# Adding two of the three chords of VectorE's exponentials in an accumulating DMA

## The chip, the cores and the metric

One core of a Trainium2 chip runs the whole program. The metric is the device time of one execution in microseconds (us). The kernel before takes 757.84 us, the median of 3 runs (757.2 to 758.05). One more execution was taken with the hardware profiler; its span, from the first to the last instruction, is 754.6 us, and every duration below comes from it.

## The reference: one transformer block

2048 tokens of width 512 pass through an attention with 32 heads of width 16 and then through a gated feed-forward layer of width 1792, each behind a layer norm and with its input added back:

```python
def _A_ref(x, wqkv, wo):
    qkv = (x @ wqkv).reshape(B, S, 3, H, Dh).transpose(2, 0, 3, 1, 4)
    q, k, v = qkv[0], qkv[1], qkv[2]
    scores = jnp.einsum("bhqd,bhkd->bhqk", q, k) * (Dh ** -0.5)
    p = _softmax(scores, axis=-1)
    o = jnp.einsum("bhqk,bhkd->bhqd", p, v)
    return o.transpose(0, 2, 1, 3).reshape(B, S, D) @ wo

def _B_ref(x, w_gate, w_up, w_down):
    h = _sigmoid(x @ w_gate) * (x @ w_up)
    return h @ w_down

h = x + _A_ref(_layernorm(x), A_wqkv, A_wo)
out = h + _B_ref(_layernorm(h), B_w_gate, B_w_up, B_w_down)
```

The heads are narrow, so the exponentials are what there is most of: 32 x 2048 x 2048 of them.

## The kernel before, and what sets its order

**Units and tiles.** The scores are computed transposed, keys on the 128 partitions and queries along the free axis. A *unit* is 128 x 512 exponentials of one head: two key tiles by 256 queries, or in the first blocks one key tile by 512 queries. There are 2048 units. A *tile* is what one step of the main loop takes from PSUM: mostly three units, one bank each. `scores(n)` (L1085) lets TensorE write the scores of tile n; four units can use four groups of 32 rows of the array at once.

**Two engines make the exponentials.** ScalarE takes two units of a tile (three where VectorE has no room) in one ACTIVATE with Exp (L1408) and writes fp16 into a run of neighbouring *slots*: 24 slots of 512 columns in the tile `PT`, and more that other buffers lend (`xb`, `PE_`, `QTb`, `xnT`). VectorE takes one unit, the last of the tile, with `dexp_first` (L1256): one TENSOR_SCALAR turns the scores into int16 numbers, the *code*, whose bits read as fp16 are a piecewise straight approximation of the exponential, a *chord*. To come closer, the code is shifted by two constants (`CHORDS`), which gives two more chords; the wanted value is chord 0 plus chord 1 plus 1.5625 times chord 2.

**Three chords are three operands.** A tile `J` of [128, 3, 2, 512] holds the three chords of two units; there are six such buffers (`QB = 6`). After every second unit `dexp_rest` makes the two other chords, each by one integer add on GpSimd (`int64_add`, L1277, four int16 at once). The sum of the three is left to TensorE: `av` (L1233) multiplies every chord by its values, one after the other into the same accumulator, chord 2 with `Vaug2`, which is `Vaug` times 1.5625. So a unit of ScalarE costs TensorE one AV unit and a unit of VectorE costs three. An AV unit is two matmuls of 17 rows by 256 columns (one of 512 in the first blocks), and four heads run on four groups of columns at once.

**Background work.** Between scores and AV, TensorE does the projections, `wo`, the gate and up matmuls (L824) and the down matmuls (L842) of the feed-forward layer; its weights `wgu` come by DMA from SP's queue, 256 KB each, two for every two blocks of 128 columns. The last part of the feed-forward layer runs after the attention; its gate and up weights go into the `J` buffers (L1495) as these come free.

**A planner writes the order.** No scheduler is at work on the chip: every engine runs its queue in the order in which the Python code emits it. The code keeps a clock for each engine (`T["P"]`, `T["A"]`, `T["D"]`, `T["G"]` for TensorE, ScalarE, VectorE, GpSimd) and gives each operation a price in ns; a unit has an `end`, and `av` takes only units whose `end` plus 60 ns has passed on TensorE's clock (L1233 and `av_ready`). Since TensorE's queue is in order, a matmul whose operand comes later on the chip than the planner supposed holds up everything behind it. VectorE gets a unit of a tile (`split`) when its clock is not too far behind ScalarE's and a `J` buffer is free.

Of the kernel before, what the change touches and what calls it, by code (L numbers as in the profile page):

```python
# [9 lines left out]
FP16 = mybir.dt.float16  # L10
BF16 = mybir.dt.bfloat16
I16 = mybir.dt.int16
I32 = mybir.dt.int32
I64 = mybir.dt.int64
ALU = mybir.AluOpType
# [12 lines left out]
CHORDS, WEIGHT = (326, -332), 1.5625  # L28
# [114 lines left out]
def kernel(  # L143
# [11 lines left out]
    nc = tc.nc  # L155
    P = 128
    S, D = A_x.shape[1], A_x.shape[2]
# [3 lines left out]
    DC = D // P  # L161
    NG = H // 4
    NP = NG // 2
    FC = F // P
    QC = 512
# [20 lines left out]
    ZOFF = 1024 * (15 - LEVEL)  # L186
# [11 lines left out]
    dvx = main.enter_context(tc.tile_pool(name="dvx", bufs=1))  # L198
# [13 lines left out]
    Vaug = const.tile([P, NT, H, VW], BF16)  # L212
    Vaug2 = const.tile([P, NT, H, VW], BF16)
# [43 lines left out]
    for b in range(0, P, 32):  # L257
        nc.vector.tensor_tensor(out=ident_bf[b:b + 32, b:b + 32], in0=ramp[b:b + 32, 0, :],
                                in1=ramp[b:b + 32, 1, :], op=ALU.is_equal)
# [296 lines left out]
    def pool(ns, fn, *deps):  # L556
        gq.append(Job(ns, fn, deps))
        job = gq[-1]
        run_pool()
        return job  # L560
# [64 lines left out]
    def flush():  # L625
        moved = True
        while moved and (dq or aq):
            moved = False
            for q, e in ((dq, "D"), (aq, "A")):
                for job in list(q):  # L630
                    if job.ready() is not None:
                        q.remove(job)
                        job.place(e)
                        moved = True
# [576 lines left out]
    def av(limit, loose=60.0, full=False):  # L1211
        busy = [st["acc"][k] for k in acc_of(*gseq[st["cur"]])[1] if st["acc"][k] is not None]
        if any(j.end is None or j.end + LAT > T["P"] + loose for j in busy):
            return 0
        uns, rows = in_rows(av_ready(loose), ahead_ready(), limit, full)
        if not uns:
            return 0
        T["P"] = max([T["P"]] + [un.end + LAT for un in uns + busy])
        for un in uns:
            qc, g, kt, j = un.u  # L1220
            dst, halves = acc_of(qc, g)
            for k in halves:
                st["acc"][k] = None
            force(("v", kt * SPAN[qc]))
            avq.remove(un)
            c = count[qc, g, j]
            count[qc, g, j] += 1
            todo[qc, g, j] -= 1
            h = 8 * (g // 2) + 2 * j + g % 2
            w = CW[qc]  # L1230
            clears = 0 in halves
            for i in range(SPAN[qc]):
                nc.tensor.matmul(dst[32 * j:32 * j + VW, 0:w], lhsT=un.v[:, kt * SPAN[qc] + i, h, :],  # L1233
                                 rhs=un.ap[:, i * w:(i + 1) * w], start=clears and c + i == 0,
                                 stop=(todo[qc, g, j] == 0 and i == SPAN[qc] - 1), tile_position=(0, 32 * j),
                                 skip_group_check=True)
        pe_time("av", MM * rows + 4 * len(uns), 128 * len(uns))
        for un in uns:
            if un.slot is not None:
                un.slot.end = T["P"] + DRAIN  # L1240
        while st["cur"] < len(gseq) and av_last() == 0:
            finish_group(*gseq[st["cur"]])
            st["cur"] += 1
        return len(uns)

    GQ, QB = 2, 6
    quads = []
    half = []

    def dexp_first(src, u, n):  # L1250
        if not half:
            half.append(dvx.tile([P, 3, GQ, QC], I16, name="J", bufs=QB))
            quads.append([])
        J = half[0]
        k = len(half) - 1
        nc.vector.tensor_scalar(out=J[:, 0, k, :], in0=src, scalar1=ZOFF, scalar2=float(-min(CHORDS)),  # L1256
                                op0=ALU.add, op1=ALU.max)
        T["D"] = max(T["D"], sc_end[n] + LAT) + 601
        todo[u[0], u[1], u[3]] += 2
        uns = [Unit(u, J[:, s, k, :].bitcast(FP16), n, None if s else T["D"] + TAIL["D"],  # L1260
                    v=Vaug2 if s == 2 else Vaug) for s in range(3)]
        avq.extend(uns)
        half.append(uns)
        quads[-1].extend(uns)
        if k == GQ - 1:
            dexp_rest()

    def dexp_rest():
        J, quad = half[0], half[1:]
        half.clear()  # L1270
        k = len(quad)

        def words(s):
            return J[:, s, 0:k, :].rearrange("p a b -> p (a b)").bitcast(I64)

        def chord64(s):
            nc.gpsimd.int64_add(words(s), words(0), CHORDS[s - 1] * (1 + 2 ** 16 + 2 ** 32 + 2 ** 48))  # L1277
            for i in range(k):
                quad[i][s].end = T["G"] + TAIL["G"]

        def chord(s):
            nc.vector.tensor_scalar(out=J[:, s, 0:k, :], in0=J[:, 0, 0:k, :], scalar1=float(CHORDS[s - 1]),
                                    scalar2=None, op0=ALU.add)
            for i in range(k):
                quad[i][s].end = T["D"] + TAIL["D"]
        on_pool = len(st["early"]) == TQ * (NQC - 1) and all(j.end is not None for j in st["early"])
        if on_pool and not st["lib"]:
            st["lib"] = True
            T["G"] += 9000.0
        for s in (1, 2):  # L1290
            if on_pool:
                pool(150 + 192 * k, lambda s=s: chord64(s), Mark(T["D"] + TAIL["D"]))
            else:
                chain.append((70 + 133 * k, lambda s=s: chord(s)))

    def want_dve(n):

        quads[:] = [q for q in quads if any(un in avq for un in q)]
        if not blocks or not late("d"):
            return False  # L1300
        busy = sum(j.ns for j in dq if j.ready() is not None) + sum(c[0] for c in chain)
        rest = group_left() / 2.8
        if not half and len(quads) >= QB:
            return False
        if busy > 1500:
            return False
        return busy + 1900 + 1100 * (GQ - len(half[1:])) <= rest * 1100
# [2 lines left out]
        def __init__(self, tile, i, early=False):  # L1310
            self.tile, self.i, self.early, self.unit, self.end = tile, i, early, None, 0.0

    NPT, NPE = 24, 14
    PT = ptp.tile([P, NPT, QC], FP16, name="pt")
    PE_ = prep.tile([P, NPE, QC], FP16, name="pe")
    slots = [Slot(PT, i) for i in range(NPT)] + [Slot(x, i, True) for x, n in (
# [14 lines left out]
    def run_of(w):  # L1331

        best = None
        for i in range(len(slots) - w + 1):
            row = slots[i:i + w]
            if row[0].tile is row[-1].tile and not any(s.unit in avq for s in row):
                end = max(s.end for s in row)
                if best is None or end < best[0]:
                    best = end, row
        return best  # L1340

    def p_slots(w):
        while True:
            best = run_of(w)
            if best is not None:
                return best
            flush()
            if av(8, 1e12) or early_on and try_bg(1e9, 1e12):
                continue
            if half and not chain:  # L1350
                dexp_rest()
            if chain:
                pop_chain()
# [20 lines left out]
    n = -1  # L1374
    while n + 1 < len(tiles):
# [16 lines left out]
        start = max(T["A"], sc_end[n] + LAT)  # L1392
        busy = sum(j.ns for j in dq if j.ready() is not None) + sum(c[0] for c in chain)
        dable = len(tl) > 1 and busy <= 1500
        split = (dable and max(T["D"], sc_end[n] + LAT) <= start + 600 and bool(half or len(quads) < QB))
        if n > N - 12:
            end = max(T["D"], sc_end[n] + LAT) + 1900 + 600 * (GQ - len(half[1:]) if half else GQ)
            split = split and end <= start + 1330 * (N - n) - 500
        if half and half[1][0].u[:2] != tl[-1][:2]:
            dexp_rest()  # L1400
            quads[:] = [q for q in quads if any(un in avq for un in q)]
            split = split and len(quads) < QB
        wa = len(tl) - split
        more_slots()
        free_at, row = p_slots(wa)
# [68 lines left out]
    ends = [PS[:, wide["base"] + i, :] for i in range(3)] + [PS[:, last + i, :] for i in range(3)]  # L1474
    hps, gu = ends[0:n], ends[n:n + 4]
    nc.vector.tensor_scalar(out=ident2[:], in0=ident_bf[:], scalar1=2.0, scalar2=None, op0=ALU.mult)
    while any(un.n < N - 1 and un.slot is not None for un in avq):
        flush()
        av(8, 1e12)
    nc.scalar.activation(out=small.tile([P, 1], FP32, name="warm")[:], in_=eps_t[:], func=ACT.Sqrt)  # L1480
# [5 lines left out]
                             start=False, stop=False)  # L1486
    T["P"] += MM * n * NP
    tw = {}
    for i in range(QB):
        t = dvx.tile([P, 3, GQ, QC], I16, name="J", bufs=QB)[:].rearrange("p a b n -> p (a b n)")  # L1490
        n = min(3 * GQ // 2, FC - len(tw))
        f = len(tw)
        w = t[:, 0:n * 2 * DC * P].bitcast(BF16).rearrange("p (k c n) -> p k c n", k=2, c=DC)
        for k in range(2):
            nc.sync.dma_start(out=w[:, k], in_=gate_v[k][:, :, f * P:(f + n) * P])  # L1495
        for m in range(n):
            tw[f + m] = w[:, :, :, m * P:(m + 1) * P]
        if len(tw) == FC:
            break

    while avq:
        flush()
# [31 lines left out]
            for job in held:  # L1534
                job.end = 0.0
    leftover(7)
    hnl = [PT[:, k, :].bitcast(BF16) for k in range(n)]
    nc.scalar.activation(out=hnl[0], in_=hps[0], func=ACT.Identity, bias=nmr[:, 0:1], scale=rstd[:, 0:1])
    nc.vector.tensor_scalar(out=hnl[1], in0=hps[1], scalar1=mv[:, 1, 0:1], scalar2=rstd[:, 1:2],
                            op0=ALU.subtract, op1=ALU.mult)  # L1540
# [73 lines left out]
```

## Time and profile before

| | value |
|---|---|
| time, median of 3 runs | 757.84 us |
| span of the profiled execution | 754.6 us |
| start until the first exponential of ScalarE | 13.1 us |
| last exponential of ScalarE starts at | 717.2 us |
| tail (last norm and feed-forward part) | from about 720 us |
| tiles of the main loop | 695 |
| units on VectorE / on ScalarE | 619 / 1429 |
| integer adds on GpSimd | 640, 603 ns each |
| DMA moved in all | 41.65 MB, mean 55 GB/s |

In the page, the share of busy time tells which engines are full; since the stages differ, the same is read for each stage from the table of windows. Groups of instructions show how long one takes, how long its engine sat idle before it and what ended that. The chain of waits is followed back from the last instruction.

### The profile page before, as it was taken

How to read it: one execution, taken by the hardware profiler on the slowest of the kernel's cores; microseconds unless marked ns; L12 is line 12 of the kernel's file. 1: busy time of each engine (PE TensorE's matmuls, PEld its weight loads, DVE VectorE, ACT ScalarE, POOL GpSimd, SP SyncE). 2: the span in 40 equal slices, each digit the busy share in tenths (PEclk: the TensorE clock that was granted, in tenths of full speed). 3: DMA queues.
4: the chain of work that ended last, by engine and by line, in shares of the span. 5: the costliest groups of instructions: out<-in, count | busy, mean ns of one | idle time of the engine just before them, and what ended most of it. 6: DMA issues, size and time to landing. Idle time of an engine off the chain costs nothing.

```text
span 754.6 us, 27232 instructions
## 1 busy us (share of the span) xinstructions
PE 718.8 (95%) x11541; PEld 347.4 (46%) x11617; DVE 621.7 (82%) x1231; ACT 709.2 (94%) x788; POOL 396.0 (52%) x709
## 2 busy tenths in 40 slices
PE   7999998889999999999999999999999999999997
PEld 3322224444454445444555454535544455445554
DVE  7988878889978898898889688977889777899743
ACT  7989989999999999999999999999999999899952
POOL 2733546666556456655645546564555446465600
PEclk9999999999999999999999999999999999999999
DMA  7000005000123003210222122201321133003160
GB/s 238 1 1 1 1 18 153 2 3 3 30 87 99 10 10 109 78 30 10 78 59 59 36 79 58 74 22 38 99 59 30 44 93 107 10 9 105 47 203 17
DMA packets 68927, 41.65 MB, mean 55 GB/s; under 512 B 3520, under 2 KB 68800, under 8 KB 68800
## 3 DMA queue, kind: packets, MB, share of 16 engines
q1 hardware_dynamic: 68512, 39.59, 17.9%
q8 instruction: 92, 1.51, 0.9%
q14 instruction: 35, 0.29, 0.1%
q10 hardware_dynamic: 288, 0.26, 0.1%
HBM read 37.75 MB, written 2.10 MB: 53 GB/s over the span
## 4 chain that ended last, share of the span: by engine, by line
PE 74%; ACT 13%; DVE 8%; issue 4%; DMA 0%; POOL 0%; DVEq 0%; ACTq 0%; POOLq 0%
PE PS L1085 24%; PE PS L1233 23%; PE PS L824 14%; ACT pt L1408 10%; PE PS L842 6%; DVE J L1256 4%; PE PS L311 2%; PE PS L316 2%; PE PS L763 1%; ACT QTb L1408 1%; DVE xs L1151 1%; ACT xnT L1408 1%; PE PS L1560 1%; DVE st L271 1%; PE PS L305 1%
## 5 line engine op out<-in xcount | busy, mean ns | idle before, releaser
L1277 POOL INT64_ADD J<-J x640 | 377.6, 603 | 305.3 <-DVE J L1256 261.4
L1408 ACT ACTIVATE pt<-PS 128x1024 f16<-128x1024 f32 (+2 forms) x517 | 517.3, 1104 | 13.3 <-PE PS L1085 5.1
L1256 DVE TENSOR_SCALAR J<-PS 128x512 int16<-128x512 f32 x619 | 413.8, 681 | 70.1 <-PE PS L1085 42.7
L1085 PE MATMUL PS<-QT,KT 32*128 32x256 bf16 (+1 forms) x3712 | 263.8, 276 | 10.9 <-ACT pt L1408 4.9
L1233 PE MATMUL PS<-J,Vaug 128*17 128x256 f16 (+1 forms) x3546 | 243.4, 279 | 3.3 <-DVE xs L1151 1.9
L1233 PE MATMUL PS<-pt,Vaug 128*17 128x256 f16 (+1 forms) x2043 | 205.0, 279 | 2.8 <-DVE xs L1151 2.3
L1233 PEld LDWEIGHTS <-Vaug 128*17 128x17 bf16 x6204 | 139.3, 90 | 91.5 <-issue 84.4
L1085 PEld LDWEIGHTS <-KT 32*128 32x128 bf16 x3840 | 89.1, 92 | 197.2 <-issue 193.8
L824 PE MATMUL PS<-xnT,wgu 128*128 128x256 bf16 x784 | 113.7, 275 | 0.1
L1408 ACT ACTIVATE xnT<-PS 128x1024 f16<-128x1024 f32 x90 | 95.0, 1080 | 0.9 <-PE PS L1085 0.7
L824 PEld LDWEIGHTS <-wgu 128*128 128x128 bf16 x784 | 63.6, 97 | 39.6 <-issue 34.2
L1233 PE MATMUL PS<-xnT,Vaug 128*17 128x256 f16 x362 | 56.4, 274 | 0.0
L842 PE MATMUL PS<-wd,hT 128*128 128x512 bf16 x169 | 51.2, 383 | 2.5 <-issue 2.5
L1151 DVE STREAM_TRANSPOSE xs<-PS 128x256 f32<-128x256 f32 (+1 forms) x60 | 27.7, 461 | 21.9 <-PE PS L1233 21.2
L854 ACT ACTIVATE th<-PS 128x512 f32<-128x512 f32 (+1 forms) x63 | 37.4, 594 | 8.4 <-DVE hT L837 6.7
L1408 ACT ACTIVATE QTb<-PS 128x1024 f16<-128x1024 f32 x40 | 42.7, 1068 | 0.5 <-PE PS L1085 0.5
L896 DVE SCALAR_TENSOR_TENSOR hT<-th,PS 128x512 bf16<-128x512 f32 x49 | 33.3, 680 | 7.3 <-PE PS L824 7.2
L1233 PE MATMUL PS<-QTb,Vaug 128*17 128x256 f16 (+1 forms) x158 | 28.4, 275 | 0.0
L1408 ACT ACTIVATE xb<-PS 128x1024 f16<-128x1024 f32 (+2 forms) x26 | 25.6, 1030 | 2.1 <-PE PS L1085 1.1
L1122 DVE TENSOR_TENSOR o<-xs,rsum 128x128 bf16<-128x128 f32 (+1 forms) x60 | 24.4, 407 | 2.1
L1408 ACT ACTIVATE pe<-PS 128x1024 f16<-128x1024 f32 (+2 forms) x22 | 21.7, 1062 | 1.7 <-PE PS L1233 1.4
L842 PEld LDWEIGHTS <-hT 128*128 128x128 bf16 x196 | 12.2, 97 | 20.8 <-issue 17.8
(128 smaller groups left out, 397.5 us busy)
## 6 DMA issues: line engine op xcount, KB each, us to landing
wgu<-in_B_w_gate_dram SPq DMA_DIRECT2D x49, 256.0 KB, 3.0
wgu<-in_B_w_up_dram SPq DMA_DIRECT2D x49, 256.0 KB, 3.5
out_dram<-ob SPq DMA_DIRECT2D x16, 128.0 KB, 2.1
wd<-in_B_w_down_dram SPq DMA_DIRECT2D x1, 1792.0 KB, 8.8
xr<-in_A_x_dram SPq DMA_DIRECT2D x14, 128.0 KB, 3.8
xb<-in_A_x_dram SPq DMA_DIRECT2D x6, 256.0 KB, 6.0
J<-in_B_w_gate_dram SPq DMA_DIRECT2D x4, 384.0 KB, 5.9
J<-in_B_w_up_dram SPq DMA_DIRECT2D x4, 384.0 KB, 7.0
```

Source lines behind the costliest of these rows:

```text
L311: nc.tensor.matmul(ps, lhsT=w_sb[:, d, p * P:(p + 1) * P], rhs=xnT[c][:, d, :], start=(d == 0), stop=(d == DC - 1))
L824: nc.tensor.matmul(ps[:, 0:PARTS[r][2]], lhsT=w[:, d, :], rhs=hn_of(r)[:, d, :], start=(d == 0), stop=(d == DC - 1))
L842: nc.tensor.matmul(ps, lhsT=hT[:, f, i * P:(i + 1) * P], rhs=wd[:, f, :], start=(f == 0), stop=(f == FC - 1))
L854: nc.scalar.activation(out=th[:, 0:ps.shape[-1]], in_=ps, func=ACT.Tanh, scale=0.5)
L896: nc.vector.scalar_tensor_tensor(out=hT[:, f:f + k, 0:w], in0=th[f][:].rearrange("p (k n) -> p k n", k=k), scalar=1.0, in1=ps2.rearrange(" ...
L1085: nc.tensor.matmul(pss[:, ui, i * CW[qc]:(i + 1) * CW[qc]], lhsT=KT[g // 2][32 * j:32 * j + 32, k * P:(k + 1) * P], rhs=q[32 * j:32 * j + ...
L1122: nc.vector.tensor_tensor(out=o2[:, 0:w // 32, DH * a:DH * a + DH], in0=xs[:, 0:w // 32, 0:DH], in1=rec.to_broadcast([P, w // 32, DH]), op ...
L1151: j = dve(650 - ns[0], lambda: nc.vector.transpose(out=xs[:, 0:w // 32, :].rearrange("p b r -> p (b r)"), in_=src), Mark(T["P"] + DRAIN), ...
L1233: nc.tensor.matmul(dst[32 * j:32 * j + VW, 0:w], lhsT=un.v[:, kt * SPAN[qc] + i, h, :], rhs=un.ap[:, i * w:(i + 1) * w], start=clears and ...
L1256: nc.vector.tensor_scalar(out=J[:, 0, k, :], in0=src, scalar1=ZOFF, scalar2=float(-min(CHORDS)), op0=ALU.add, op1=ALU.max)
L1277: nc.gpsimd.int64_add(words(s), words(0), CHORDS[s - 1] * (1 + 2 ** 16 + 2 ** 32 + 2 ** 48))
L1408: ex = nc.scalar.activation(out=pt, in_=pss[:, 0:wa, :], func=ACT.Exp, scale=AS)
```

## The change

VectorE now gathers the codes of *three* units (`GQ = 3`) in a tile `C`, of which there are four (`QT_ = 4`). Once three are there (or fewer at the end of a group), `dexp_rest` takes two runs of slots from the general slots, of which `PT` now has 48, and has GpSimd do three things in this order:

1. `int64_add` of the code and the first constant into the first run, three units at once (L1303),
2. a DMA that GpSimd issues, with `accum_op=add`: the first run += the code, both read as fp16 (L1310). After it the run holds chord 0 + chord 1,
3. `int64_add` of the code and the second constant into the second run: chord 2.

So TensorE has two AV units for a unit of VectorE, where it had three: the sum with `Vaug`, chord 2 with `Vaug2`. The planner is told that the issue holds GpSimd for 1000 ns (`DMA_ISSUE`) and that the sum is there 3000 ns after that (`DMA_LAT`); an add is priced 288 + 158 ns for each unit, where it was 150 + 192. A new rule, `room_dve`, gives VectorE a unit when enough slots are free and the fourth code tile back has been read by its DMA. The weights of the last feed-forward part, which lay in the `J` buffers, go into runs of four general slots (`take`), two blocks of columns at a time, in 14 DMAs of 256 KB; they were 8 of 384 KB and 2 of 256 KB. Before the first matmuls of the tail, `av` now runs until of the units of earlier tiles only third chords (`Vaug2`) are left.

```diff
-    GQ, QB = 2, 6
-    quads = []
+    GQ, QT_ = 3, 4
+    DMA_ISSUE, DMA_LAT = 1000.0, 3000.0
     half = []
+    codes = []
+
+    def room_dve():
+        busy = sum(s.unit in avq for s in slots)
+        if len(slots) - busy < 2 * (len(half[1:]) + 1) + 6:
+            return False
+        if half or len(codes) < QT_:
+            return True
+        e = codes[-QT_].end
+        return e is not None and e <= T["D"] + 300
...
-        uns = [Unit(u, J[:, s, k, :].bitcast(FP16), n, None if s else T["D"] + TAIL["D"],
-                    v=Vaug2 if s == 2 else Vaug) for s in range(3)]
+        uns = [Unit(u, None, n, None, v=Vaug2 if s else Vaug) for s in range(2)]
...
+        J, free = [], []
+        for s in range(2):
+            at, row = p_slots(k)
+            J.append(row[0].tile[:, row[0].i:row[0].i + k, :])
+            free.append(at)
...
+        def chord64(s):
+            nc.gpsimd.int64_add(words(J[s].bitcast(I16)), words(C[:, 0:k, :]),
+                                CHORDS[s] * (1 + 2 ** 16 + 2 ** 32 + 2 ** 48))
...
+        def add_dma():
+            nc.gpsimd.dma_start(out=J[0], in_=C[:, 0:k, :].bitcast(FP16), accum_op=ALU.add)
+            code.end = T["G"] + DMA_LAT
+            for i in range(k):
+                quad[i][0].end = T["G"] + DMA_LAT
...
+        if on_pool:
+            pool(288 + 158 * k, lambda: chord64(0), Mark(max(m, free[0])))
+            pool(DMA_ISSUE, add_dma)
+            pool(288 + 158 * k, lambda: chord64(1), Mark(max(m, free[1])))
...
-    NPT, NPE = 24, 14
+    NPT, NPE = 48, 14
...
-    while any(un.n < N - 1 and un.slot is not None for un in avq):
+    while any(un.n < N - 1 and un.v is not Vaug2 for un in avq):
...
+    hrow = take(2)
+    for f in range(0, FC, 2):
+        row = take(4)
+        w = row[0].tile[:, row[0].i:row[0].i + 4, :].bitcast(BF16).rearrange(
+            "p s n -> p (s n)").rearrange("p (k c n) -> p k c n", k=2, c=DC)
         for k in range(2):
-            nc.sync.dma_start(out=w[:, k], in_=gate_v[k][:, :, f * P:(f + n) * P])
-        for m in range(n):
+            nc.sync.dma_start(out=w[:, k], in_=gate_v[k][:, :, f * P:(f + 2) * P])
+        for m in range(2):
             tw[f + m] = w[:, :, :, m * P:(m + 1) * P]
```

## The prediction

> **What bounds the kernel now.** I read the page's busy table first, then the windows stage by stage, then the groups with the idle time before them, then the waits.
>
> ```profile
> span 754.6 us, 27232 instructions
> PE 718.8 (95%) x11541; PEld 347.4 (46%) x11617; DVE 621.7 (82%) x1231; ACT 709.2 (94%) x788; POOL 396.0 (52%) x709
> ...
> L1277 POOL INT64_ADD J<-J x640 | 377.6, 603 | 305.3 <-DVE J L1256 261.4
> L1408 ACT ACTIVATE pt<-PS 128x1024 f16<-128x1024 f32 (+2 forms) x517 | 517.3, 1104 | 13.3 <-PE PS L1085 5.1
> L1256 DVE TENSOR_SCALAR J<-PS 128x512 int16<-128x512 f32 x619 | 413.8, 681 | 70.1 <-PE PS L1085 42.7
> ```
>
> ```profile
> 200.00:300.00 100.00, 98.10 (x1730) 50.30 (x1740) 86.65 (x170) 97.66 (x109) 56.32 (x98) 1.00 0.22 63
> 300.00:400.00 100.00, 98.25 (x1745) 48.21 (x1750) 88.25 (x183) 98.11 (x107) 56.54 (x96) 1.00 0.17 50
> 400.00:500.00 100.00, 98.01 (x1752) 50.21 (x1760) 87.07 (x171) 97.83 (x109) 57.40 (x97) 1.00 0.21 60
> ```
>
> A row of the second fence is a stretch, its length, and the busy us of TensorE, weight loads, VectorE, ScalarE and GpSimd. From 200 to 500 us TensorE *and* ScalarE are both at 98%, GpSimd at 56%. So the loop has two full engines: relief of TensorE alone is worth only what ScalarE still waits for it. GpSimd waits for VectorE's codes, not the other way round (261.4 us).
>
> Forms kept apart, and one stretch of the timeline:
>
> ```profile
> L1408 ACT ACTIVATE pt<-PS 128x1024 f16<-128x1024 f32 x468 | 455.7, 1075 | 5.3 <-PE PS L1085 3.7 <-PE PS L1233 0.2
> L1408 ACT ACTIVATE pt<-PS 128x1536 f16<-128x1536 f32 x44 | 64.6, 1477 | 7.9 <-issue 4.1 <-PE PS L1233 2.1 <-PE PS L1085 1.3
> ...
> 401.66 0.78 PEld L1233 LDWEIGHTS <-Vaug 128*17 128x17 bf16 x32 [0.21 <-issue]
> ...
> 403.40 1.23 POOL L1277 INT64_ADD J<-J  x2 [1.91 <-DVE J L1256]
> ```
>
> A third unit costs ScalarE 1.477 - 1.075 = 0.40 us. AV matmuls of 256 columns follow each other at 0.78 / 32 = 24.4 ns. The last code before 403.40 ended at 403.23 on VectorE: GpSimd starts 0.17 us after what it waits for.
>
> ```profile
> wgu<-in_B_w_gate_dram SPq DMA_DIRECT2D x49, 256.0 KB, 3.0
> wgu<-in_B_w_up_dram SPq DMA_DIRECT2D x49, 256.0 KB, 3.5
> out_dram<-ob SPq DMA_DIRECT2D x16, 128.0 KB, 2.1
> wd<-in_B_w_down_dram SPq DMA_DIRECT2D x1, 1792.0 KB, 8.8
> ```
>
> These are issues with KB and us to landing. None comes from GpSimd, none adds, and none ends in SBUF from SBUF: what the change lives on isn't in this trace.
>
> **What the Trainium skill says.** "DMA: Bandwidth & Descriptors", Anatomy of one DMA: a DMA that GpSimd issues takes about 2.0 us plus bytes at 436 GB/s; 384 KB (three units) gives 2.0 + 0.9 = 2.9 us as an estimate. The same page, Latency and other measured facts: GpSimd's path has its first byte after about 1 us. "Collectives: The Full Stack", The bandwidth ceiling: an adding DMA reads two sources on the same ring and so runs at about half the rate; then 2.0 + 1.8 = 3.8 us. "SBUF — State Buffer", Who interferes with whom: a VectorE instruction with two SBUF inputs contends with GpSimd's reads. The trace agrees with the size of the first only roughly (SP's loads: 2.1 us for 128 KB, 8.8 for 1792 KB); it shows neither of the second and third; GpSimd's adds reach 825 ns beside a median of 613, as the fourth would have it.
>
> **The change part by part.** Counts are of the two programs as built; the main loop has 695 tiles in both.
>
> *ScalarE.* VectorE takes 643 units in place of 619. ScalarE's exponentials go from 636 of two units, 49 of three and 10 of one to 658, 26 and 11: 24 units less at 0.40 us, 9.7 us off a full engine. This is sure as far as the order goes.
>
> *TensorE.* AV units fall from 2048 + 2 x 619 = 3286 to 2048 + 643 = 2691: 1098 matmuls of 256 columns and 46 of 512 less, at 24.4 and 49 ns 29 us. Part of it is filled with waiting and with matmuls that only keep the array busy (20 before, 44 after, by the order). Worth to the end: ScalarE's exponentials (L1408, all destinations) wait 11.6 us for matmuls by the view of that line (7.6 for scores, 4.0 for AV); I take a third, 4 us (between 0 and 11.6).
>
> *VectorE.* 24 codes x 0.68 = 16 us on an engine that is at 87%; nothing waits. Two chords at L1282 go. *Tail weights:* 14 issues for 10 on SP at 0.37 to 0.51 us each, 2 us more, into slots that are long free; before, the first was issued at 714.7 and the first use is at 730.65. Nothing, unless the first slips by 8 us. *Start of the tail:* the sum of the last trio must be multiplied before the first tail matmul; before, TensorE was there 1.3 us after the last exponential (718.66 to 719.94); now a DMA of about 4 us begins near that exponential. 1.4 us (0 to 3). Sum so far: -9.7 - 4 + 1.4 = -12.3 us.
>
> *GpSimd.* 480 adds and 240 DMAs (188 of three units, 27 of two, 25 of one). The shortest add is 0.39 us (one unit), the usual 0.613 (two), so 0.17 + 0.22 a unit and 0.83 for three; all adds come to 82 + 283 = 365 us. An issue at the planner's and the skill's 1.0 us, with 0.17 for the semaphore between the add and the DMA that reads its result, comes to 281. Together 646 us of the about 656 in which codes come: GpSimd, at 56%, becomes nearly full. In the planner's prices it is 581.
>
> *The new wait.* A sum that is late stops TensorE, with the next tile's scores queued behind the matmul and both exponential engines behind those. The planner's margins can be read while the order is built: between the moment at which it takes a sum for landed and the place of its first matmul lie at most 0.1 us for 25 of 240, 0.3 for 51, 0.6 for 88, 1.0 for 133 and 2.0 for 182; the median is 0.89. In tiles: the first use comes a median of six tiles after the trio's last code, six times 1.01 us. How late are sums against the planner? Start of the add 0.17 against 0.06: +0.11. The add 0.83 against 0.76: +0.07. Semaphore before the DMA, +0.15. Behind the previous trio's second add on a nearly full queue, +0.3 (0 to 0.6). From issue to landing the planner has 4.0; one pass by this trace is 2.1 + 256 x (6.7 / 1664) = 3.1, with the second read 4.1 to 4.7, by the skill 2.9 to 3.8: I take 3.85, -0.15 (-1.1 to +0.7). Weight loads share the 16 DMA engines, 98 of them at some 3 us: about a third of the sums meet one and lose 0.9: +0.27. Sum +0.75 us, between -0.2 and +1.7.
>
> Going through the 240 in order (a wait also delays later codes, so the next trio's margin stays; a DMA already in flight gains by it) gives waits of 5 us in all for 0.2 us late, 12 for 0.4, 21 for 0.6, 28.5 for 0.75, 43 for 1.0, 83 for 1.6. Spare time on TensorE gives back little, since ScalarE has none; I take off 2. Span: 754.6 - 12.3 + 26.5 = 768.8. The median of the runs lies 3.2 above the span: 772.
>
> **The rivals.**
> *The sums come in time (faster).* The skill's 2.9 us, or short waits on GpSimd. 0.2 us late or less: -12.3 + 3 gives 748.5. For it: the planner's prices elsewhere are close (its add of 604 ns for two units is what the trace has). Against it: it has no price for the semaphore on GpSimd. It decides from under 0.4 us of lateness.
> *GpSimd becomes the bound (slower).* The same change, another place: if an issue holds it 1.4 us rather than 1.0, its sum is 742 us, from 34 to 776, then the tail of 34 us: about 810 with what lies around it. For it: 646 of 656 already. It decides from about 1.1 us for an issue. Code tiles then run out and VectorE waits for GpSimd.
> *Hidden anyway.* Lateness near 0.4 us: gain and waits cancel, 757 to 759.
> That the change doesn't do what it says is excluded by the order: 240 adding DMAs, and no VectorE unit with three operands.
>
> **How the numbers follow.** About 0.2% (1.5 us) is what a measurement of this kernel can tell from no change. Sums late by 0.45 us or more (slower): 0.43, the forecast, 772, its own range 760 to 800. GpSimd the bound: 0.18, 800 to 830. In time: 0.33, 744 to 755. Cancelled: 0.06. Slower 0.61, same 0.06, faster 0.33. Both signs hold much, so the range reaches from 746 to 808.
>
> **What would show it.** After: two-unit exponentials at the same 1075 ns but tiles further apart than 1.01 us; among the waits, L1233's matmuls for the DMA into `pt` with 20 to 35 us in all, and ScalarE waiting for TensorE's scores by about as much; INT64_ADD 480 times at about 0.8 us; GpSimd above 80% busy with the issues counted; DMA issues of 384 KB from GpSimd at about 3.9 us to landing. Wrong if TensorE hardly waits for these DMAs (then the faster rival holds), if VectorE waits for GpSimd or for code tiles (then GpSimd is the bound), or if landing takes under 3.3 us from the start of the issue.

## The result, and the profile after

The changed kernel takes 844.4 us (median of 4 runs, 837.8 to 853.6) beside 757.8 us for the kernel before: ratio 1.112, 95% interval 1.107 to 1.118. The slowest of the four, 853.6 us, is over 1.5% above the fastest, counts as slow and is left out of the ratio; the median of the other three is 841.2 us. Differences below are taken from 844.4 us; from 841.2 us they would be 3 us smaller. The forecast was 772 us. The direction was right; the loss was 86.6 us and not 14.

The page of the kernel after is of that slowest execution; its mean granted clock is 0.947, that of the others 0.957 to 0.973. It has these lines, among them those that answer to the lines shown of before:

```profile
span 851.6 us, 25409 instructions
...
PE 759.7 (89%) x10493; PEld 331.0 (39%) x10493; DVE 680.1 (80%) x1253; ACT 712.4 (84%) x788; POOL 600.8 (71%) x789
...
PEclk9999987898999979999988999989998999999999
...
q0 software_dynamic: 34560, 84.29, 56.3%
...
L1446 ACT ACTIVATE pt<-PS 128x1024 f16<-128x1024 f32 (+2 forms) x563 | 553.1, 1049 | 88.1 <-PE PS L1085 75.7
L1268 DVE TENSOR_SCALAR C<-PS 128x512 int16<-128x512 f32 x643 | 429.7, 681 | 104.5 <-PE PS L1085 84.2
L1303 POOL INT64_ADD pt<-C x432 | 401.6, 999 | 114.8 <-DVE C L1268 91.0
...
L1233 PE MATMUL PS<-pt,Vaug 128*17 128x256 f16 (+1 forms) x4420 | 233.5, 289 | 49.9 <-DMA pt<-C 39.2
L1310 POOL DMA_DIRECT2D pt<-C x216 | 189.2, 876 | 69.4 <-POOL pt L1303 55.4
...
L1122 DVE TENSOR_TENSOR o<-xs,rsum 128x128 bf16<-128x128 f32 (+1 forms) x60 | 50.1, 835 | 2.1
...
L324 DVE TENSOR_SCALAR QT<-qd,mask 128x512 bf16<-128x512 bf16 x28 | 23.7, 854 | 0.0
...
pt<-C POOLq DMA_DIRECT2D x175, 384.0 KB, 4.4
```

The windows of the loop after, with the same columns as before (TensorE, weight loads, VectorE, ScalarE, GpSimd, then granted clock, DMA share and GB/s):

```profile
200.00:300.00 100.00, 87.82 (x1411) 39.91 (x1407) 86.29 (x168) 87.89 (x97) 77.52 (x95) 0.97 0.79 153
300.00:400.00 100.00, 86.67 (x1310) 38.92 (x1304) 86.72 (x154) 84.65 (x92) 73.71 (x92) 0.95 0.77 150
400.00:500.00 100.00, 91.32 (x1323) 40.52 (x1324) 80.33 (x146) 84.15 (x91) 72.45 (x92) 0.93 0.73 148
```

Before, TensorE and ScalarE were at 98% here. Now no engine is full: ScalarE, whose two-unit exponentials are no longer than before (1.04 us for 1.08), waits 75.7 us for scores, and GpSimd stands at about 75%. Over the whole span TensorE's idle time grew from 36 to 92 us, and its busy time from 719 to 760 us, though it has fewer matmuls. Time went into waits that go round in a ring, so the page's longest waits name victims as well as causes.

Two places stand out. The first was forecast: L1233's matmuls wait 39.2 us for the DMA that adds into `pt`. The second was not. The groups of VectorE in the kernel before have these two rows:

```profile
L1122 DVE TENSOR_TENSOR o<-xs,rsum 128x128 bf16<-128x128 f32 (+1 forms) x60 | 24.4, 407 | 2.1
...
L324 DVE TENSOR_SCALAR QT<-qd,mask 128x512 bf16<-128x512 bf16 x28 | 11.7, 423 | 0.1
```

The same instructions on the same shapes last twice as long after: 407 to 835 ns and 423 to 854 ns, 25.7 + 12.0 = 37.7 us in all. The codes at L1268, which read PSUM, stay at 681 ns; the 24 added ones are 16.3 us, and nearly all that is left of VectorE's growth (621.7 to 680.1 us) lies in two other groups from SBUF to SBUF. One stretch of the timeline after shows what such an instruction meets, and who pays (start, duration, engine, line; in brackets the idle time before it and what ended it):

```profile
153.69 0.87 POOL L1310 DMA_DIRECT2D pt<-C  x1 [0.30 <-POOL pt L1303]
...
154.23 2.17 DVE L1122 TENSOR_TENSOR o<-xs,rsum 128x128 bf16<-128x128 f32 x1
154.30 1.94 POOL L1303 INT64_ADD pt<-C  x2
...
156.32 0.68 DVE L1268 TENSOR_SCALAR C<-PS 128x512 int16<-128x512 f32 x1
156.54 0.88 POOL L1310 DMA_DIRECT2D pt<-C  x1 [0.30 <-POOL pt L1303]
...
157.05 0.58 PE L1085 MATMUL PS<-QT,KT 32*128 32x256 bf16 x2 [1.01 <-DVE C L1268]
...
159.37 1.02 ACT L1446 ACTIVATE pt<-PS 128x1024 f16<-128x1024 f32 x1 [1.74 <-PE PS L1085]
```

L1122 takes 0.29 us alone (the view of its tile gives 291 ns as the shortest in both kernels). Here it begins beside GpSimd's DMA issue, lies through two adds, and ends at 156.40, 0.16 us after the second. VectorE's next code starts at 156.32, TensorE waits 1.01 us for it before it can write new scores, and ScalarE, two microseconds on, 1.74 us for scores. Of the 90 instructions of L1122 and L324, 48 lie beside one or more INT64_ADDs and end 120 to 170 ns after the last of them that is over (30 in the kernel before); 52 last over 450 ns (23 before). A few that lie within an add are not held. What TensorE pays, its waits tell (who waits for whom, us in total, times, longest). The first row is from the kernel after, the second from a version with shorter holds (e13 below); in the kernel before, scores waited for VectorE for 0.2 us in all.

```profile
PE PS L1085 <- DVE C L1268: 12.6, 22, 1.4
...
PE PS L1085 <- DVE C L1268: 3.3, 6, 1.0
```

The Trainium skill, "SBUF — State Buffer", SBUF: two separate sides, calls the port pair that VectorE and GpSimd share "an exclusive lock, not a bandwidth split". The ends fit a lock. In 37 of the 52 the record of an add begins first; in the other 15, as in the stretch shown, VectorE's record begins before any add's, though beside a DMA issue, and it is VectorE that waits all the same.

A third thing comes with the pauses. The granted clock of TensorE falls to half in 17 stretches, all but the last (3.9 us, at the end) of 3.4 us or multiples of it, 92.7 us in all (before: one, 5.1 us, at the end). In the 3.4 us ahead of each of the first 16, TensorE was busy for 24 to 68% of the time. The skill's "TensorE: Matmul & The Clock Gate", What's actually happening, gives the window as 3413 ns, and the half clock after an idle one. The length agrees. The idle window doesn't: no pause of TensorE in this execution is longer than 2.9 us. 92.7 us at half speed are at most 46 us of work lost. From their mean granted clock the three faster executions have 45 to 72 us at half clock, as an estimate.

### The profile page after: what moved, and what is told of

Same layout as the page of the kernel before. It is cut to its first block, busy times and chain, and to the rows that moved or that the text cites. A ratio compares the mean times of both kernels' runs of the same rounds, so it can differ in the third digit from the quotient of the medians.

```text
span 851.6 us, 25409 instructions
## 1 busy us (share of the span) xinstructions
PE 759.7 (89%) x10493; PEld 331.0 (39%) x10493; DVE 680.1 (80%) x1253; ACT 712.4 (84%) x788; POOL 600.8 (71%) x789
## 5 line engine op out<-in xcount | busy, mean ns | idle before, releaser
L1446 ACT ACTIVATE pt<-PS 128x1024 f16<-128x1024 f32 (+2 forms) x563 | 553.1, 1049 | 88.1 <-PE PS L1085 75.7
L1268 DVE TENSOR_SCALAR C<-PS 128x512 int16<-128x512 f32 x643 | 429.7, 681 | 104.5 <-PE PS L1085 84.2
L1303 POOL INT64_ADD pt<-C x432 | 401.6, 999 | 114.8 <-DVE C L1268 91.0
L1233 PE MATMUL PS<-pt,Vaug 128*17 128x256 f16 (+1 forms) x4420 | 233.5, 289 | 49.9 <-DMA pt<-C 39.2
L1310 POOL DMA_DIRECT2D pt<-C x216 | 189.2, 876 | 69.4 <-POOL pt L1303 55.4
L1233 PEld LDWEIGHTS <-Vaug 128*17 128x17 bf16 x5060 | 114.9, 92 | 153.4 <-issue 123.5
L1446 ACT ACTIVATE xnT<-PS 128x1024 f16<-128x1024 f32 (+1 forms) x58 | 60.7, 1062 | 11.0 <-PE PS L1085 10.5
L1233 PE MATMUL PS<-xnT,Vaug 128*17 128x256 f16 x368 | 51.9, 284 | 3.4 <-DMA xnT<-C 3.4
L1122 DVE TENSOR_TENSOR o<-xs,rsum 128x128 bf16<-128x128 f32 (+1 forms) x60 | 50.1, 835 | 2.1
L1233 PE MATMUL PS<-QTb,Vaug 128*17 128x256 f16 (+1 forms) x166 | 29.5, 294 | 0.0
L1303 POOL INT64_ADD xnT<-C x29 | 27.1, 934 | 1.5 <-DVE C L1268 0.9
L324 DVE TENSOR_SCALAR QT<-qd,mask 128x512 bf16<-128x512 bf16 x28 | 23.7, 854 | 0.0
```

The source lines that it names most:

```text
L1122: nc.vector.tensor_tensor(out=o2[:, 0:w // 32, DH * a:DH * a + DH], in0=xs[:, 0:w // 32, 0:DH], in1=rec.to_broadcast([P, w // 32, DH]), op ...
L1268: nc.vector.tensor_scalar(out=C[:, k, :], in0=src, scalar1=ZOFF, scalar2=float(-min(CHORDS)), op0=ALU.add, op1=ALU.max)
L1303: nc.gpsimd.int64_add(words(J[s].bitcast(I16)), words(C[:, 0:k, :]), CHORDS[s] * (1 + 2 ** 16 + 2 ** 32 + 2 ** 48))
L1310: nc.gpsimd.dma_start(out=J[0], in_=C[:, 0:k, :].bitcast(FP16), accum_op=ALU.add)
L1446: ex = nc.scalar.activation(out=pt, in_=pss[:, 0:wa, :], func=ACT.Exp, scale=AS)
```

## The experiments

There are two suspects: sums that come late, and GpSimd's longer work, which holds up VectorE. Theory A in the expectations is always that the lateness of the adding DMA alone makes the loss; the others are told in each. Ratios are to the kernel before on the same chip, which lay between 757.0 and 757.9 us. The last three columns are of one profiled execution each.

| run | us | ratio (95%) | L1233 waits for the DMA into `pt`, us | L1122, ns | half clock, us |
|---|---|---|---|---|---|
| before | 757.8 | 1 | none | 407 | 5.1 |
| after | 844.4 | 1.112 (1.107 to 1.118) | 39.2 | 835 | 92.7 |
| e1 plan 4500 | 808.2 | 1.068 (1.066 to 1.070) | 22.6 | 698 | 34.0 |
| e2 plan 6000, six code tiles | 828.1 | 1.092 (1.089 to 1.095) | 10.5 | 770 | 54.5 |
| e3 copy (one run) | 775.2 | | 7.2 | 659 | 34.7 |
| e4 no weight loads (one run) | 825.1 | | 22.5 | 914 | 67.2 |
| e5 control, 18 slots | 774.6 | 1.023 (1.021 to 1.025) | none | 388 | 5.0 |
| e6 control + side adding DMAs | 809.1 | 1.069 (1.065 to 1.072) | none | 587 | 16.6 |
| e7 control + side copies by SP | 775.5 | 1.024 (1.022 to 1.027) | none | 388 | 8.5 |
| e9 control + GpSimd adds | 810.0 | 1.070 (1.068 to 1.072) | none | 581 | 18.3 |
| e10 e9, planned | 803.9 | 1.062 (1.060 to 1.064) | none | 639 | 20.4 |
| e11 e6, planned | 793.1 | 1.048 (1.046 to 1.050) | none | 608 | 5.0 |
| e12 issue last, 4500 | 789.8 | 1.044 (1.041 to 1.046) | 18.3 | 480 | 35.4 |
| e13 issue last, 3000 | 811.5 | 1.069 (1.065 to 1.073) | 43.6 | 598 | 56.1 |
| e14 issue last, 5500 | 800.0 | 1.057 (1.055 to 1.059) | 12.5 | 482 | 31.5 |
| e15 issue last, pairs | 814.2 | 1.076 (1.074 to 1.078) | 7.3 | 570 | 62.4 |
| e16 issue last, copy | 775.1 | 1.024 (1.022 to 1.026) | 7.1 | 438 | 35.3 |
| e17 before, 30 slots | 761.9 | 1.006 (1.005 to 1.007) | none | 423 | 4.6 |
| e18 issue last, plain end | 780.5 | 1.031 (1.029 to 1.032) | 10.0 | 496 | 25.0 |

**Is it lateness alone? e1 and e2.** The planner takes a sum for landed later, and so lays its matmuls later; e2 also gives two more code tiles and, for their room, six slots fewer.

```diff
-    DMA_ISSUE, DMA_LAT = 1000.0, 3000.0
+    DMA_ISSUE, DMA_LAT = 1000.0, 4500.0
```
```diff
-    GQ, QT_ = 3, 4
-    DMA_ISSUE, DMA_LAT = 1000.0, 3000.0
+    GQ, QT_ = 3, 6
+    DMA_ISSUE, DMA_LAT = 1000.0, 6000.0
...
-    NPT, NPE = 48, 14
+    NPT, NPE = 42, 14
```

> Only the planner's DMA_LAT is 4500 ns in place of 3000; 643 units on VectorE as in the changed kernel, every sum's first matmul stands later in TensorE's order. Theory A (sums later than the planner thinks stop TensorE, and its clock drops in the pauses): most of the some 60 us of TensorE's waits for these DMAs go, the granted clock rises from 0.95-0.97 to over 0.98, time 755 to 790. Theory B (GpSimd holds VectorE and itself back[...]): waits for DMAs fall but the time stays over 820.

> DMA_LAT 6000 ns, six code tiles in place of four so that VectorE keeps its units (640), 42 slots in place of 48. Theory A: nearly all waits of TensorE for the DMAs are gone, clock over 0.99, time 744 to 765. Theory B: over 815 still, with VectorE's L1122 and L324 at over 800 ns.

e1 gives 36 us back: 808.2. The waits for the DMA fall from 39.2 to 22.6 us and the half clock from 92.7 to 34.0 us. e2 brings those waits to 10.5 us (with those for other tiles than `pt`, 17.2 in place of 44.9) and is slower again, 828.1. So lateness is real, and it is not all: with some 60% of the waits for the DMA gone, 70 us of loss remain. e2 changed three numbers at once, so why it is slower than e1 is not settled.

**What does the adding cost? e3.** The same issue, as a copy; it leaves the first chord out of the sum.

```diff
-            nc.gpsimd.dma_start(out=J[0], in_=C[:, 0:k, :].bitcast(FP16), accum_op=ALU.add)
+            nc.gpsimd.dma_start(out=J[0], in_=C[:, 0:k, :].bitcast(FP16))
```

> The DMA copies the code onto the run and doesn't add to it (the sum then lacks chord 0). If the second read of the adding DMA makes it late: landing of 384 KB falls from 4.4 us to about 3.5, the queue's share of the DMA engines from 56% to about 30%, and the time by 20 to 60 us. If the fixed part of GpSimd's path or GpSimd's own instructions do it: landing over 4.1 us and the time within 15 us of the changed kernel.

775.2 us. In the page of e3:

```profile
L1303 POOL INT64_ADD pt<-C x432 | 332.4, 776 | 120.7 <-DVE C L1268 85.1
...
L1310 POOL DMA_DIRECT2D pt<-C x216 | 120.0, 556 | 69.3 <-POOL pt L1303 54.0
...
pt<-C POOLq DMA_DIRECT2D x175, 384.0 KB, 2.9
```

Not only the landing is shorter (2.9 for 4.4 us). The issue takes GpSimd 556 ns for 876, and the adds that lie partly beside it 776 ns for 999. Everything that either theory blames became smaller at once, so this run does not tell them apart.

**Do weight loads get in the way? e4.** Gate and up weights are loaded for the first two pairs of blocks only.

```diff
+    kept = {}
...
-        w = fw.tile([P, 2, DC, 2 * P], BF16, name="wgu", bufs=2)
+        if f // 2 % 2 in kept:
+            return kept[f // 2 % 2]
+        w = kept[f // 2 % 2] = fw.tile([P, 2, DC, 2 * P], BF16, name="wgu", bufs=2)
```

> The feed-forward weights are loaded only for the first two pairs of blocks and used for all (94 loads of 256 KB left out, so the feed-forward result is another). If sharing the DMA engines with these loads makes the sums late: landing falls to about 3.8 us, its longest from 8.3 to under 5.5, the time to under 810. If not: landing within 0.2 us of 4.4 and the time over 825.

825.1 us in a single run, where the runs of after reach down to 837.8; landing 4.1 for 4.4 us, the longest still 8.7 us. By its time this is the second expectation, by the landing (0.3 us less) neither: a minor part.

**Where nobody waits for the DMA: e5, e6, e7.** To the kernel before, transfers are added that nothing in the computation uses. Room is taken from the general slots, hence the control e5 with the tiles alone. e7 has `nc.sync` and no `accum_op`.

```diff
+    dummy = [dvx.tile([P, GQ * QC], FP16, name=f"dummy{i}") for i in range(3)]
+    def side():
+        st["dum"] += 1
+        nc.gpsimd.dma_start(out=dummy[st["dum"] % 3][:], in_=KT[0][:, 0:GQ * QC].bitcast(FP16), accum_op=ALU.add)
...
                 pool(150 + 192 * k, lambda s=s: chord64(s), Mark(T["D"] + TAIL["D"]))
+                if s == 1 and k == GQ:
+                    pool(0, side)
...
-    NPT, NPE = 24, 14
+    NPT, NPE = 18, 14
```

> The kernel before with 18 general slots in place of 24, the room taken by three tiles that nothing reads or writes after the start: the control of the next two runs. Both theories: 757 to 766 us; VectorE's L1122 at 0.41 us as before.

> The control with one adding DMA of two units (256 KB) issued by GpSimd after every second pair of adds, from keys that never change into three idle tiles; no instruction of the computation waits for it, so nothing is late through it. Theory A (lateness of the added chords is all): within 6 us of the control, VectorE's L1122 and L324 unchanged. Theory B (GpSimd's adds and issues, back to back, hold up VectorE's instructions that go from SBUF to SBUF, and with them codes, scores and exponentials): L1122 from 0.41 us to 0.65 or more, L324 likewise, and 10 to 40 us over the control. Theory C (the traffic itself slows loads): weight loads at 4 to 5 us, and the next run slows as much as this one.

> The same transfers in the same number and size as plain copies issued by SP, so that GpSimd issues nothing: the traffic without GpSimd's part (and without the addition's second read). Theory A: within 6 us of the control. Theory B: within 4 us of the control, L1122 at 0.41 us. Theory C: slower than the control, by about as much as the adding DMAs were.

The control takes 774.6 us, more than I had expected: six slots were worth 17 us. Beside it, 293 copies of 256 KB issued by SP cost 1 us (775.5) and the weight loads land as before; plain traffic of that amount is free. The adding DMAs issued by GpSimd cost 34.5 us (809.1), though nobody waits for them. From the page of e6:

```profile
L1285 POOL INT64_ADD J<-J x656 | 546.2, 1084 | 90.5 <-DVE J L1264 73.2
...
L1254 POOL DMA_DIRECT2D dummy<-KT x293 | 345.2, 1180 | 5.2 <-issue 3.9
L1233 PE MATMUL PS<-J,Vaug 128*17 128x256 f16 (+1 forms) x3564 | 258.5, 281 | 20.7 <-POOL J L1285 15.4
...
L1122 DVE TENSOR_TENSOR o<-xs,rsum 128x128 bf16<-128x128 f32 (+1 forms) x60 | 35.2, 587 | 2.1
```

GpSimd, busy for 399 us in the control (records that overlap counted once), is so for 657. L1122 is held (388 to 587 ns), and some ordinary chords come late: L1233 waits 15.4 us for GpSimd.

**GpSimd's time alone: e9, e10, e11.** In place of the DMA one more INT64_ADD on an idle tile, so that GpSimd is busy for about as long (661 us) and nothing is transferred. In e10 and e11 the planner counts the added time.

```diff
-        nc.gpsimd.dma_start(out=dummy[st["dum"] % 3][:], in_=KT[0][:, 0:GQ * QC].bitcast(FP16), accum_op=ALU.add)
+        nc.gpsimd.int64_add(dummy[0][:, 0:1792].bitcast(I64), dummy[0][:, 0:1792].bitcast(I64), 1)
```
```diff
-                    pool(0, side)
+                    pool(950, side)
```

> The control (18 slots, 774.6 us in that run) with one more INT64_ADD of 128x1792 two-byte numbers on GpSimd after every second pair of adds, from an idle tile into itself, some 0.9 us, so that GpSimd is occupied for about as long as in the run with the side adding DMAs (662 us) but no transfer is made and nothing is issued. Theory B (GpSimd's occupied time and its holds of VectorE): 800 to 815 us, the 34 us of that run come back whole, L1122 at 0.55 us or more. Theory D (what costs is the issue or the adding transfer itself): at most 785 us.

> The same, and the planner counts 950 ns for each of the added instructions, so that it doesn't lay the sums of the chords before GpSimd can have them. Theory B1 (the cost is chords that GpSimd delivers later than planned): TensorE's waits for GpSimd vanish and the time is 775 to 785 us. Theory B2 (the cost is VectorE held up by GpSimd): 795 us or more, L1122 at 0.55 us or more as without the plan.

> The run with the side adding DMAs (809.1 us), with 1150 ns counted for each issue. Theory B1: 775 to 787 us. Theory B2: 800 us or more. Theory D: as much above the planned run of GpSimd's adds alone as above the unplanned one.

e9 gives the same loss with no transfer at all: 810.0 us, 35.4 over the control.

```profile
L1285 POOL INT64_ADD J<-J x656 | 383.0, 594 | 91.6 <-DVE J L1264 88.8
L1233 PE MATMUL PS<-J,Vaug 128*17 128x256 f16 (+1 forms) x3564 | 258.9, 281 | 19.6 <-POOL J L1285 13.2
...
L1254 POOL INT64_ADD dummy<-dummy x293 | 274.5, 937 | 0.0
...
L1122 DVE TENSOR_TENSOR o<-xs,rsum 128x128 bf16<-128x128 f32 (+1 forms) x60 | 34.9, 581 | 2.1
```

When the planner knows of it, TensorE no longer waits for GpSimd, but only 6 of the 35 us come back (803.9): late chords are the small part, and VectorE stays held (L1122 at 639 ns, VectorE busy 659.1 us beside 627.6 in the control, nearly all of it in instructions from SBUF to SBUF, and TensorE's waits for VectorE 27.3 us beside 12.5). With the issues planned 16 of 34.5 us come back (793.1), more than either theory said. VectorE is busy for 646.5 us there, which fits that an issue holds it up less than an add; no run shows it apart. The 787 to 800 us between the two expectations of e11 are where it fell.

**Taking the hold away: e8.** L1122's multiplication goes to GpSimd, with the plan of e1.

```diff
-            nc.vector.tensor_tensor(out=o2[:, 0:w // 32, DH * a:DH * a + DH], in0=xs[:, 0:w // 32, 0:DH],
+            nc.gpsimd.tensor_tensor(out=o2[:, 0:w // 32, DH * a:DH * a + DH], in0=xs[:, 0:w // 32, 0:DH],
...
-        j = st["xs"] = dve(690 - ns[1], norm, j)
+        j = dve(190, norm, j)
+        j = st["xs"] = pool(700 if w == QC else 450, scale, j)
```

> The changed kernel with the planner's 4500 ns for a transfer (808.2 us in that run) and the multiplication of L1122 moved from VectorE to GpSimd, behind GpSimd's adds in its queue. Theory A: 805 to 812 us, since the waits for the DMA are as before. Theory B: some 25 us of VectorE's held time goes (60 instructions at 0.70 us against 0.29 unheld), exponentials keep their pace better, and the time falls to 785 to 800 us.

1551 us (ratio 2.05, 2.04 to 2.05), which no theory had. GpSimd's groups there:

```profile
L1308 POOL INT64_ADD pt<-C x425 | 391.6, 1019 | 342.7 <-issue 256.6 <-DVE C L1273 43.2 <-ACT pt L1451 24.6
...
L1126 POOL TENSOR_TENSOR o<-xs,rsum 128x128 bf16<-128x128 f32 (+1 forms) x60 | 24.4, 407 | 432.6 <-issue 345.2 <-DVE C L1273 71.8 <-DVE st L271 7.2
```

"issue" is idle time that no release ends: 345.2 us before the 60 multiplications and 256.6 before the adds, together 10 us each time GpSimd passes from INT64_ADD to another operation and back. At each such passage the trace has a pair of MODIFY_POOL_CONFIG records, 234 in this run where the kernels before and after have four. So this run says nothing for or against the held VectorE.

**Making the holds shorter in the changed kernel: e12 to e15.** GpSimd's three instructions of a trio in another order:

```diff
             pool(288 + 158 * k, lambda: chord64(0), Mark(max(m, free[0])))
-            pool(DMA_ISSUE, add_dma)
             pool(288 + 158 * k, lambda: chord64(1), Mark(max(m, free[1])))
+            pool(DMA_ISSUE, add_dma)
```

> The changed kernel with the planner's 4500 ns (808.2 us in that run) and GpSimd's three instructions of a trio in the order add, add, issue in place of add, issue, add: the issue no longer lies between two adds, and each sum is issued one add later, which the planner counts. Theory B2 (held VectorE): L1122 at most 0.60 us in place of 0.70, and 795 to 803 us. Theory A: 806 to 815 us, since the sums come no earlier.

> The changed kernel with nothing but the order of GpSimd's three instructions of a trio altered: add, add, issue. The two parts are additive: the issue last takes 18 us off with the plan of 4500 ns (808.2 to 789.8), so 844 falls to some 826 us (820 to 832), VectorE's L1122 at about 0.5 us in place of 0.84. Lateness decides alone: 840 us or more, since each sum is now issued one add later.

e13 is this edit alone: 811.5 us, 33 us less than after. GpSimd's timeline in e13:

```profile
403.62 1.62 POOL L1303 INT64_ADD pt<-C  x2 [1.23 <-DVE C L1268]
405.19 0.86 POOL L1310 DMA_DIRECT2D pt<-C  x1
406.78 1.62 POOL L1303 INT64_ADD pt<-C  x2 [0.73 <-PE PS L1085]
```

After had 0.30 us of idle time before each issue, which waits for the add just ahead of it; here the second add fills that time. Adds fall from 999 to 841 ns, GpSimd is busy for 576 in place of 601 us, L1122 falls to 598 ns and VectorE's busy time from 680.1 to 652.6 us. The waits for the DMA did not fall (43.6 us), so this gain is not lateness; what fell are the waits of scores for VectorE, from 15.4 to 3.3 us in all, and the half clock with them, from 92.7 to 56.1 us. So the clock has a part in this gain. With the plan of 4500 ns as well (e12) it is 789.8 us. The two edits are worth 33 and 36 us alone and 55 together. In e12 the planner also gives VectorE 619 units, as many as before the change, in place of 641 in e13; that is part of what a longer plan does.

e14 has 5500.0 for 4500.0 in e12; e15 has this:

```diff
-    GQ, QT_ = 3, 4
+    GQ, QT_ = 2, 6
```

> The issue last and the planner's 5500 ns. If what is left in the run of 789.8 us is lateness (TensorE still waits 18.3 us for the DMA there, and 35.4 us lie at half clock): those waits fall under 8 us and the time to 765 to 778 us. If it is the room that longer plans take (codes and slots held longer): 786 to 800 us, as the plan of 6000 ns gave 828 against 808 in the order of the change.

> The issue last, 4500 ns, and two units a transfer in place of three (256 KB, six code tiles of two): landing nearer 3.9 than 4.7 us, so that the waits for the DMA fall below 10 us, but half as many issues again. Lateness: 775 to 786 us. GpSimd's occupancy (each issue about as long for two units as for three, 1.18 us in the side run): 795 to 815 us.

A longer plan still (e14) takes waits away but moves work: VectorE gets 587 units in place of 619, ScalarE the others, and the time is 800 us. Its profiled execution was the fastest of five (791.6 us, the others 799.9 or more), so its row in the table tells less of the median. In pairs (e15) the waits for the DMA fall to 7.3 us and the time rises to 814: GpSimd is busy for 670 us, as long as in e6 or a little longer. That is the second theory's side of the expectation.

e16 is e12 with the edit of e3:

> The issue last, 4500 ns, and the DMA copies the code over the first chord in place of adding it (the output lacks that chord's part). If the adding costs through its landing time and nothing else: landing 2.9 to 3.1 us, no wait for the DMA, 757 to 770 us. If what is left lies elsewhere (slots, VectorE): 775 us or more.

The copy is worth 15 us here (775.1), where in the order of the change it was 69. So most of what the adding cost there goes with the order and the plan, be it through lateness or through holds.

**The rest: e17, e18.** The first edit is to the kernel before, the second to e12.

```diff
-    GQ, QB = 2, 6
+    GQ, QB = 2, 5
...
-    NPT, NPE = 24, 14
+    NPT, NPE = 30, 14
```
```diff
-        if on_pool:
+        if on_pool and st["n"] < N - 14:
```

> The kernel before with five tiles of codes and chords in place of six and 30 general slots in place of 24, in the same room. If slots bound it (six fewer cost 17 us): 745 to 755 us. If it has enough of them and the sixth tile is what VectorE's codes need: 762 us or more. Neither: within 0.3% of 757.

> The issue last, the plan of 4500 ns, and in the last fourteen tiles VectorE makes both chords and adds them itself, so that no transfer is in flight when the tail begins. The tail's part: from 48.0 us between the last exponential's start and the end to 39 to 42, and 789.8 us falls to 780 to 785. If VectorE's own additions (some 1.8 us a trio) delay the last exponentials as much: within 3 us of 789.8.

e18 brings the stretch from the last exponential's start to the end from 48.0 to 35.6 us and the time to 780.5: the tail was 9 of the 32 us that e12 lost. e17, six slots more for one tile of chords less, is 0.6% slower than before, so that trade gains nothing. No version beat the kernel before.

## Why the forecast had the direction and missed the size

*"VectorE: 24 codes x 0.68 = 16 us on an engine that is at 87%; nothing waits."* This step failed. It counted the codes added, rightly (16.3 us), and not what GpSimd's longer work does to the rest of VectorE's queue. L1122 and L324 took 37.7 us more, VectorE's busy time grew by 58.4 us, and TensorE's scores waited 15.4 us for VectorE in place of 0.2. The skill's section on who interferes with whom was cited and priced at nothing. On the kernel before, GpSimd's time alone costs 35 us (e9, of which 6 are late chords, e10); on the changed kernel an order with shorter holds gives 33 us back (e13, which also spares GpSimd 25 us). The miss was 72 us. That GpSimd's time costs this much though nobody waits for its results was shown on the kernel before; how much of the changed kernel's loss it is was not measured apart. That it acts through held VectorE instructions is read from their durations and ends and from what scores wait for, since the one run that moved them away (e8) was spoilt by another cost.

*Sums late by 0.75 us, waits of 28.5 us.* The mechanism was right, the size too small, and this is the other half of the miss. The adding DMA landed at 4.4 us (4.6 on the mean) and not at 3.85 with 0.27 for weight loads, inside the bounds given, and spread from 2.6 to 8.3; the issue came 0.30 us after the add and not 0.17. As an estimate, these two make the sums 1.3 us late, and the prediction's own list (43 us of waits at 1.0, 83 at 1.6) then gives about 63. Waits for it by L1233 were 39.2 us on `pt` and 5.7 on other tiles; with those before its LDWEIGHTS, in part the same time, 53.0 us. Put into its sum in place of 28.5, that makes some 797 us; the 47 us from there to 844 are about what is left for the holds and the clock. A plan with 1.5 us more gives back 36 us (e1), 22 with the issue last (e13 to e12, which also has 22 units fewer on VectorE). Sharing with weight loads was a small term of it, as forecast: without them the landing is 0.3 us shorter (e4).

*The clock.* No step had it. With the pauses of TensorE came 92.7 us at half clock in the profiled execution. It enlarges both losses; no run changed the clock alone, and its own share stays open. Pauses don't tell all of it: in e15, two of nine stretches follow 3.4 us in which TensorE was busy for 83 and 89%. Nor does the loss need it: e11 lies 18.6 us over its control with 5.0 us at half clock, as many as there.

*GpSimd: 646 us, nearly full.* That GpSimd would not be the bound was right, but not the working: an issue took 0.88 us and not 1.0, an add 1.0 on the mean and not 0.83, records overlap, and it was busy for 601 us, 71% of the span and not over 80%. A sign named for that rival was there in small: VectorE waited 10.7 us for GpSimd in all, mostly for code tiles. The rival named the wrong harm: GpSimd need not be full to cost time. It was held to decide above 1.1 us an issue; e9 shows 35 us of loss at 82%.

*ScalarE -9.7, TensorE -4.* The units went as counted (three-unit exponentials into `pt` fell from 44 to 20), yet ScalarE's relief was worth nothing, since ScalarE waited 75.7 us for scores in place of 5.1. The rival "in time, 748.5" would have needed more than a short landing: with copies that land in 2.9 us, and 11.6 us of waits for them left, it is still 775.

*Tail +1.4.* Measured 40.9 for 37.4 us from the last exponential's start, +3.5; with the issue last it grows to 48.0 (e12), and e18, where no transfer is in flight at the end, has 35.6.

What stays open is the remaining 23 us between e18 and the kernel before; L1233 still waits 10.0 us for the DMA there, and 25.0 us lie at half clock.

## What to carry to other kernels

Work moved to an engine with time to spare is free only if it blocks nobody while it runs: look for the instructions of other engines whose mean duration differs from their shortest, and expect them to grow with the time for which that engine will be busy. In a loop with two full engines, a new producer needs its real landing time in the plan, with its spread, since pauses can be paid a second time in the clock. Before adding a term for traffic, put it beside the old kernel with nobody waiting: here plain copies cost 1 us, and adding DMAs that GpSimd issued 34, as much as GpSimd's time without any transfer.

## What the runs showed of the hardware

- VectorE instructions from SBUF to SBUF (two inputs, or 128x512 bf16 by a scalar) that meet GpSimd's INT64_ADDs can be held until 0.12 to 0.17 us after the end of one of them: 0.29 us becomes up to 2.17 (48 of 90 end so in the kernel after). Codes, which read PSUM, stay at 0.68 us. With a DMA issue between the two adds L1122 takes 835 ns on the mean, with the issue behind both 598.
- The half clock of TensorE followed stretches of 3.4 us in which it was still busy for 24 to 68% of the time, with no pause over 2.9 us.
- An adding DMA of 384 KB from SBUF to SBUF lands in 4.4 us, a copy in 2.9; its issue holds GpSimd for 876 and 556 ns.
- GpSimd stands 0.30 us between its own add and the issue of the DMA that reads the result.
- GpSimd loses 10 us in passing from INT64_ADD to a TENSOR_TENSOR and back, with a pair of MODIFY_POOL_CONFIG records each way (e8).
- 293 copies of 256 KB issued by SP, with the hardware queue's share raised from 17.4% to 43.9% of the DMA engines, cost a kernel at 52 GB/s of memory traffic 1 us.
